# Four moves in a hand-written instruction order: gated lows, weight scales, first nested pieces, value rows

## The chip, the cores and the metric

The kernel runs on one core of one Trainium2 chip. A core has five engines that work beside each other: TensorE (PE, matmuls), VectorE (DVE), ScalarE (ACT), GpSimd (POOL) and SyncE (SP, which issues the transfers here). Each takes its instructions in program order and waits by semaphores for the others. The metric is the time of one execution on the device, in microseconds (us); lower is better.

## What is computed

A token-wise gate mixes an attention with memory and a gated feed-forward network, over the same input of 2048 tokens with 576 features:

```python
x = A_x                                              # (1, 2048, 576)
g = _sigmoid((x * gate_w).sum(-1, keepdims=True))
a = _A_ref(x, A_wq, A_wk, A_wv, A_wo, A_beta)        # 32 heads of 18, 4 segments of 512
b = (_gelu(x @ w_gate) * (x @ w_up)) @ w_down        # 576 -> 4608 -> 576
return g * a + (1 - g) * b

# inside _A_ref, per segment s, with phi(t) = t + 1 for t > 0, exp(t) otherwise:
p = softmax(qs @ ks.T * scale + mask)                # 512 x 512 per head
o = gh * ((phi(qs) @ M) / (phi(qs) @ z + 1e-6)) + (1 - gh) * (p @ vs)   # gh = sigmoid(beta), per head
M = M + phi(ks).T @ vs
z = z + phi(ks).sum(over tokens)
```

All inputs are float32. The kernel keeps each float32 operand as a pair of float16, a high and a low half, and multiplies high by high, high by low and low by high.

## The kernel before

The order of the instructions on PE, DVE, ACT and POOL is the order in which the kernel writes them; no scheduler moves anything. So a line of code that stands later is issued later on its engine, and everything behind it on that engine waits with it.

The kernel has three parts. First come the **projections**: for each of four chunks of 512 tokens (`s` 0 to 3), nine products for queries and keys (`project(s, j)`, 14 matmuls each, `chain_w`) and the rows of the values (`vrows`, evicted by `put_rows`). In chunk 0 the weights' pairs are made beside them: `make_qk` and `make_v` scale a weight, take its high half on ACT and its low half on DVE (L115) or on POOL (L606). What `put_columns` and `put_rows` leave in the list `later` is issued by `finish_later`.

Then come 72 **steps** (`step(v)`), four to a block (`fb` the block, `i4` the step in it). A step computes half of the gate and up products of one slice of 128 hidden features for 1024 tokens, by a product scheme with seven instead of eight products (names such as A11, S1, S4, written by `product` and `rest` into the accumulator banks V, X and Y); in half of them one of the products is itself split the same way (`nest`, pieces 0 to 3, and `nest_last`). Between the products stand, for one head and one half of the tokens, the scores (`scores`, L1158, evicted by `put`, which adds the mask and takes the maximum, L1161), the powers (`powers`: ACT takes the exponential and a high half `ph`, POOL a low half `pb`, L1179, and SP issues two transposing transfers into `pt`, L1182), the values (`values`, L1196, which reads `pt`) and `normalize`; and the down products of the block before (`down`, one chain of six matmuls at L1243 into a bank, evicted by DVE at L1251). A step's eight chains are `early` 0 to 4 and `late` 0 to 2. Blocks after the first take 75.6 us each, from about 262 us on. A **tail** with the output projection ends the kernel.

Four places concern the change:

- `hidden_pair` turns a gated product (`gl` or `hold`) into a pair `hh`: ACT takes the high half (L1273), POOL the low half (L1281). In a block's fourth step the low halves are only put on a list and are issued by `hidden_lows`, which stands behind `powers`. The tile `hold` is written again by the copy at L1381, after piece 0 of the nest.
- `scales(fb + 1)` sums the squares of the next block's weights over partitions by a matmul with ones (`sums`, L94) into a bank, and DVE makes powers of two of them (L265 to L272); `scales_out` goes on with six small operations on POOL (L278 to L286). The banks called `dn` are two, and taken in turn by the scores, the down chains and `sums`.
- In step 3 (the last of the first block) the four pieces of the next block's first nest stand in one step.
- In chunk 0, `make_v(2)` and `make_v(3)` go by POOL, and the three small operations on `gh` (L958 to L960) stand on DVE in the third projection.

Of the kernel before, what the change touches and what calls it, by code (L numbers as in the profile page):

```python
# [13 lines left out]
OP = mybir.AluOpType  # L14
# [4 lines left out]
P = 128  # L19
# [24 lines left out]
def kernel(ctx: ExitStack, tc: tile.TileContext, xs, wqk, wv, wo, wgu, wd, beta, out):  # L44
# [76 lines left out]
    def outscale(c, i):  # L121
        o = slice(i, i + 1)
        pool.tensor_scalar(al[:, c, o], wis[:, i if i < 2 else 4 :][:, :1], xis[:, c : c + 1], None, OP.mult)
        if i != 1:
            pool.tensor_scalar(nal[:, c, i // 2 : i // 2 + 1], al[:, c, o], -1.0, None, OP.mult)
        if i == 0:
            pool.tensor_scalar(esc[:, 0, c : c + 1], al[:, c, o], al[:, c, o], SCALE * 2.0**28, OP.mult, OP.mult)
            pool.tensor_scalar(esc[:, 1, c : c + 1], esc[:, 0, c : c + 1], -1.0, None, OP.mult)
        if i == 1:
            pool.tensor_scalar(gha[:, c], gh[:, 1], al[:, c, o], 2.0**14, OP.mult, OP.mult)  # L130

    x_raw = {}
    x16 = {}
# [266 lines left out]

    def chain_w(o, w, x, between=None):

        todo = [(k, a, 4 * b + k) for k in range(4) for a, b in ((0, 0), (0, 1), (1, 0))] + [(4, a, 8) for a in (0, 1)]
        if between:
            todo.sort(key=lambda t: (t[0] == 4, t[2] >= 4, t[1]))
        for n, (k, a, i) in enumerate(todo):
            if between and n == 8:
                between()
            pe.matmul(o, w(k, a), x[:, i], start=n == 0, stop=n == 13)  # L409

# [141 lines left out]
    with tc.tile_pool(name="prj", bufs=2, side="right", reuse_waits="tile") as pp:  # L552
# [45 lines left out]
        def make_v(k):  # L598
            t = W[9 + k] = pa.tile([P, 2, D + 2], F16, name="wv", bufs=5)
            r, sc = raw_v[:, k], wsc[:, 1:2]  # L600
            if k not in (2, 3):
                pair_of(t, r, sc)
                return
            act.activation(r, r, AF.Copy, scale=sc)
            act.activation(t[:, 0], r, AF.Copy)
            pool.tensor_tensor(t[:, 1], r, t[:, 0], OP.subtract)  # L606
# [12 lines left out]

        def project(s, j, between=None):  # L620
            w = W[j]
            i = j % 4
            if s == 0:
                i = (1, 1, 3, 4, 4, 1, 0, 3, 1)[j]
            pr = bank("dn", 2) if s and j == 0 or i == 4 else bank("G") if i == 0 else bank("U") if i == 3 else bank("st", 2)
            chain_w(pr, lambda k, a: w[:, a, k * P : (k + 1) * P], x16[s], between)
            return s, j, pr

        def put_columns(s, j, pr):
# [163 lines left out]
        with tc.manual_schedule(engines=ORDERED):  # L793
# [128 lines left out]
            def beside_products(s, j):  # L922
# [4 lines left out]
                if s == 0:  # L927
                    if j == 0:
                        put_rows(0, 0, 0, va[0], usc, 1.0)
                        make_qk(3, pair_high)  # L930
                        finish_later()
                        make_qk(3, pair_low)
                        fold_squares(0, 0)
                    if j == 1:
                        scale_sum(0, wst[:, 10:19], va[3][:, 420:])
                        turns.update(of=3, n=4)
                        dve.tensor_scalar(unq, wis[:, 4:5], 2.0**-14, wsc[:, 0:1], OP.mult, OP.mult)
                        outscale(0, 0)
                        outscale(0, 2)
                        fold_squares(0, 1)  # L940
                        make_qk(4)
                        put_rows(0, 1, 0, va[1], usc, 1.0)
                        finish_later()
                    if j == 4:
                        make_qk(7, pair_high)
                        finish_later()
                        make_qk(7, pair_low)
                    elif 2 <= j < 6:
                        make_qk(j + 3)
                    if j == 2:  # L950
                        for q in (2, 3):
                            put_rows(0, q, 0, va[q], usc, 1.0)
                        for q in FIRST:
                            put_rows(0, q, 1, vb[q], usc, 1.0)
                        finish_later()
                        x_raw.pop(0)
                    if j == 2:
                        dve.tensor_scalar(gh[:, 1], gh[:, 1], 1.0, None, OP.add)  # L958
                        dve.reciprocal(gh[:, 0], gh[:, 1])
                        dve.tensor_scalar(gh[:, 1], gh[:, 0], -1.0, 1.0, OP.mult, OP.add)  # L960
                    if j == 4:
                        outscale(0, 1)
                    if 1 <= j < 5:
                        make_v(j - 1)
                    if j == 4:
                        make_v(4)
                if s < 3:
# [46 lines left out]
            for s in range(4):  # L1014
# [26 lines left out]
                for j in range(9):  # L1041
                    if j == 1 and s:
                        make_gate(s)
                    if s and j == 0:
                        memory_scale(p)
                    pr = project(s, j, None if s or j else lambda: first_words(vb, 1, 4, FIRST))
                    if s and j == 0:
# [16 lines left out]
                    beside_products(s, j)  # L1064
                    finish_later()
                    if (s, j) == (1, 3):
                        make_gate(0)
                    if s == 0 and j >= 6:
                        q = j - 5
                        pv = vrows(0, q, 1)  # L1070
                        put_rows(0, q, 1, *pv)
                    if s == 3 and j == 6:
# [19 lines left out]
    with tc.tile_pool(name="keep", bufs=2, side="right", reuse_waits="tile") as kp, ExitStack() as tail:  # L1092
# [174 lines left out]

        lows = []

        def hidden_pair(f, c, t, wait=False):  # L1270
            slot = hh_slot[f, c] = hh_free.pop(0)
            hh = hp[f, c] = hh_tile(slot)
            act.activation(hh[:, 0], t, AF.Copy)  # L1273
            lows.append((hh, t))
            if not wait:
                hidden_lows()

        def hidden_lows():
            while lows:
                hh, t = lows.pop(0)  # L1280
                pool.tensor_tensor(hh[:, 1], t, hh[:, 0], OP.subtract)  # L1281

# [22 lines left out]
        def weights_nest(fb, i4, at):  # L1305
# [12 lines left out]
            if i4 == 2 and at == 2:  # L1318
                for i in (2,) if fb else (2, 3):
                    nest_pairs(fb + 1, i, "hl")  # L1320
            if i4 == 3 and at == 0:
                hidden_lows()
                if fb:
                    nest_pairs(fb + 1, 3, "hl")

# [76 lines left out]

        def end_pair(wait=False):

            for i, g in enumerate(ends):
                if len(g) < 5:
                    hidden(*g)
                if i == 0:
                    for qi in (1, 0):
                        if puts:  # L1410
                            puts[max(puts)](qi)
            for f, c, o, g, *_ in ends:
                hidden_pair(f, c, g, wait)
            ends.clear()

        def step(v):
# [13 lines left out]
            x1, x2_, t = x16[c], x16[e], xt[p]  # L1430
            end_pair(i4 == 3 and fb > 0)
            if v == 3:
# [9 lines left out]
            elif i4 < 2:  # L1442
                if on(k - 2):
                    values(2 * k - 3)
                V, g1 = nested.pop((fb, p)), gl_tile()
            else:
                V, g1 = bank("V"), holds[p]
                product(V, f, A22, x2_, 0, 4, True)
            X, Y = bank("G"), bank("U")
            product(X, f, A11, x1, 0, 4, True)  # L1450
            if fb and i4 < 2:
                nest_last(fb, V, p)
# [12 lines left out]
            if v == 1:  # L1465
                scale_result()
            one = 2 if fb and i4 < 2 else 1
            some(fb - 1, early[:one])
            put(2 * k - 1, 2)
# [50 lines left out]
            rest(X, f, U4, x1, (0,) if fb else (0, 1))  # L1520
            if v == 3:
                nest(at, 0)
            some(fb - 1, early[2:3])
            if fb and i4 == 1:
                scales(fb + 1)
                scales_out(fb + 1)
            product(Y, f, S1, t, 0, 2)
            rest(Y, f, G4, x2_, (0,) if fb else (0, 1))
            if v == 3:
                nest(at, 1)  # L1530
            if fb:
# [10 lines left out]
            some(fb - 1, early[3:])  # L1542
            put(2 * k, 3)
            if on(k - 2) and not on(k):
                normalize(k - 2)
            if not fb:
                hidden(f, c, X, g0)
                hidden_pair(f, c, g0, v == 2)
                if v < 3:
# [7 lines left out]
            if v == 3:  # L1557
                nest(at, 2)
            rest(Y, f, UG, x2_, (0,) if fb else (0, 1))
# [22 lines left out]
            if on(k):  # L1582
                puts[2 * k + 1] = scores(2 * k + 1)
            nest(at, 3)
            ends.append((f, e, Y, g1))
            if v == 3:
                nest_pairs_x(1, 1)
            weights_nest(fb, i4, 2)
            if v == 2:
                hidden_lows()  # L1590
            load_head(k + 2)
# [262 lines left out]
```

## Time and profile before

| | |
|---|---|
| three runs | 1621.01, 1622.6, 1622.64 us (median 1622.6) |
| the profiled execution | 1622.98 us, of which the span of the profile is 1621.3 us |
| granted TensorE clock, mean | 0.996 |
| busy: PE, DVE, ACT, POOL | 1564.1, 1275.8, 1211.2, 1124.0 us |
| transfers | 209.97 MB, 130 GB/s on the mean |

Times in the rows of a profile are microseconds from the start of the span. A row of the timeline gives the start, the length, the engine, the line of the kernel, the operation, the tile written and the tiles read, and in brackets how long the engine had waited and what released it; "x2" stands for two instructions of the same kind behind each other. A row of the waits gives the engine and its line, what it waited for, the sum, how often, and the longest.

### The profile page before, as it was taken

How to read it: one execution, taken by the hardware profiler on the slowest of the kernel's cores; microseconds unless marked ns; L12 is line 12 of the kernel's file. 1: busy time of each engine (PE TensorE's matmuls, PEld its weight loads, DVE VectorE, ACT ScalarE, POOL GpSimd, SP SyncE). 2: the span in 40 equal slices, each digit the busy share in tenths (PEclk: the TensorE clock that was granted, in tenths of full speed). 3: DMA queues.
4: the chain of work that ended last, by engine and by line, in shares of the span. 5: the costliest groups of instructions: out<-in, count | busy, mean ns of one | idle time of the engine just before them, and what ended most of it. 6: DMA issues, size and time to landing. Idle time of an engine off the chain costs nothing.

```text
span 1621.3 us, 33956 instructions
## 1 busy us (share of the span) xinstructions
PE 1564.1 (96%) x12220; PEld 957.2 (59%) x12220; DVE 1275.8 (79%) x3254; ACT 1211.2 (75%) x2059; POOL 1124.0 (69%) x1220
## 2 busy tenths in 40 slices
PE   9999999999999999999999999999999999999999
PEld 5665655555555555556555555556555556556577
DVE  6778976878878787878787878778787878787665
ACT  7567544888888887888788888887888878787421
POOL 5245555867776867686776777776868676776597
PEclk9999999999999999999999999999999999999999
DMA  6633331576867687776667677777687777764546
GB/s 222 209 129 130 123 115 55 116 131 120 145 116 148 128 123 136 121 129 130 126 119 128 121 144 121 139 121 151 119 139 130 133 127 134 121 120 95 111 85 172
DMA packets 472833, 209.97 MB, mean 130 GB/s; under 512 B 427688, under 2 KB 437416, under 8 KB 472152
## 3 DMA queue, kind: packets, MB, share of 16 engines
q1 hardware_dynamic: 472664, 207.80, 64.3%
q8 instruction: 96, 1.57, 0.4%
q14 instruction: 73, 0.60, 0.1%
HBM read 91.87 MB, written 27.26 MB: 73 GB/s over the span
## 4 chain that ended last, share of the span: by engine, by line
PE 71%; DVE 9%; POOL 8%; ACT 5%; issue 3%; DMA 3%; SPq 0%; DVEq 0%; POOLq 0%; ACTq 0%
PE dn L1243 19%; PE U L529 12%; PE G L529 8%; PE V L529 5%; PE V L1365 4%; PE pv L1196 4%; POOL pb L1179 3%; PE st L409 2%; PE dn L416 2%; DVE pb L270 1%; PE U L1289 1%; PE G L1294 1%; PE G L409 1%; PE U L409 1%; ACT ph L1178 1%
## 5 line engine op out<-in xcount | busy, mean ns | idle before, releaser
L1179 POOL TENSOR_TENSOR pb<-pb,ph 128x896 f16<-128x896 f32 (+1 forms) x256 | 368.7, 1440 | 311.7 <-ACT ph L1178 301.7
L529 PEld LDWEIGHTS <-pairg 128*128 128x128 f16 x2592 | 248.3, 98 | 260.2 <-issue 14.0
L1243 PE MATMUL dn<-paird,hhr 128*128 128x288 f16 x2124 | 327.9, 288 | 4.7 <-DVE mx L1161 4.1
L1177 ACT ACTIVATE pb<-pb,mb,esc 128x512 f32<-128x512 f32 (+3 forms) x512 | 304.9, 642 | 5.3
L1251 DVE SCALAR_TENSOR_TENSOR acc<-dn,ev,acc 128x288 f32<-128x288 f32 x534 | 263.7, 513 | 39.1 <-PE dn L1243 33.1
L1243 PEld LDWEIGHTS <-hhr 128*128 128x128 f16 x2160 | 208.3, 98 | 90.3 <-issue 19.6
L529 PE MATMUL U<-xt,pairg 128*128 128x512 f16 x864 | 209.8, 379 | 1.3 <-DVE gl L1501 1.3
L529 PE MATMUL G<-x,pairg 128*128 128x512 f16 x864 | 209.9, 379 | 0.8 <-DVE gl L1266 0.6
L1243 PE MATMUL dn<-paird,hhd 128*128 128x288 f16 x1272 | 206.3, 288 | 1.9 <-DVE mx L1161 1.9
L1178 ACT ACTIVATE ph<-pb 128x896 f16<-128x896 f32 (+1 forms) x256 | 188.5, 736 | 8.1
L342 POOL TENSOR_TENSOR pairg<-raw,pairg 128x384 f16<-128x384 f32 (+2 forms) x144 | 157.6, 1115 | 14.1 <-ACT pairg L338 14.1
L1161 DVE CUSTOM_DVE_ANT_0 pb<-st,mask 128x512 f32<-128x512 f32 (+1 forms) x256 | 157.0, 613 | 1.1 <-DMA pt<-pb 1.1
L1243 PEld LDWEIGHTS <-hhd 128*128 128x128 f16 x1296 | 125.4, 98 | 52.1 <-issue 8.5
L1365 PE MATMUL V<-xt,nest 128*128 128x256 f16 x714 | 107.1, 275 | 38.0 <-DVE hold L1381 37.7
L1172 ACT ACTIVATE mb<-mx,esc 128x4 f32<-128x4 f32 x128 | 37.1, 289 | 115.6 <-DVE mx L1161 115.6
L1161 DVE CUSTOM_DVE_ANT_0 pb<-dn,mask 128x256 f32<-128x256 f32 (+1 forms) x192 | 66.9, 373 | 67.1 <-PE dn L1158 65.1
L1365 PEld LDWEIGHTS <-nest 128*128 128x128 f16 x714 | 65.0, 98 | 73.1 <-issue 50.2
L529 PE MATMUL U<-x,pairg 128*128 128x512 f16 x432 | 105.0, 379 | 1.6 <-DVE gl L1536 1.6
L529 PE MATMUL V<-x,pairg 128*128 128x512 f16 x426 | 103.9, 380 | 0.0
L1284 ACT ACTIVATE gl<-gl,sc 128x512 f32<-128x512 f32 x110 | 75.8, 715 | 31.2 <-DVE gl L1536 19.4
L1281 POOL TENSOR_TENSOR hhr<-gl,hhr 128x512 f16<-128x512 f32 x67 | 78.4, 1180 | 14.6 <-ACT hhr L1273 14.6
L1196 PEld LDWEIGHTS <-pt 128*128 128x128 f16 x2560 | 84.2, 96 | 6.5 <-DMA pt<-pb 0.5
(364 smaller groups left out, 3142.2 us busy)
## 6 DMA issues: line engine op xcount, KB each, us to landing
raw<-in_wgu_dram SPq DMA_DIRECT2D x36, 640.0 KB
rawd<-in_wd_dram SPq DMA_DIRECT2D x36, 288.0 KB
qt<-qk SPq DMA_DIRECT2D x132, 72.0 KB
kt<-qk SPq DMA_DIRECT2D x132, 72.0 KB
qk<-stage SPq DMA_DIRECT2D x36, 256.0 KB
qt<-qk SPq DMA_DIRECT2D x132, 36.0 KB
kt<-qk SPq DMA_DIRECT2D x132, 36.0 KB
vp<-vstage SPq DMA_DIRECT2D x16, 296.0 KB
```

What stands on the lines that cost most here:

```text
L342: pool.tensor_tensor(spot(f, *p, 1), raw_g[f][:, p[0] : p[1]], spot(f, *p, 0), OP.subtract)
L529: pe.matmul(o, w[:, i, (a + k) * P : (a + k + 1) * P], x[:, b + k], start=start and k == 0 and i == 0 and b == h, stop=k == 1 and i == 1, ...
L1161: dve.tensor_tensor_reduce(scored(a, qi), out[qi], mask[:, L - (qi + 1) * P :], 1.0, -3e38, OP.add, OP.max, mx[a][:, qi : qi + 1])
L1177: act.activation(r, r, AF.Exp, bias=b[:, qi : qi + 1], scale=esc[:, 0, c : c + 1])
L1178: act.activation(h[:, cols], p, AF.Copy)
L1179: pool.tensor_tensor(low[:, cols], p, h[:, cols], OP.subtract)
L1196: pe.matmul(ov, pr[:, 10 * i + COL[qi] // P + kb], v[:, 4 * e + kb, c0 : c0 + VC], start=kb == 0 and i == 0, stop=kb == qi and i == 1)
L1243: pe.matmul(o[:, :NH], hh[:, a, q * P : (q + 1) * P], w[:, b, n * NH : (n + 1) * NH], start=i == 0, stop=i == 5)
L1251: dve.scalar_tensor_tensor(av, o[:, :NH], ev, av, OP.mult, OP.add)
L1281: pool.tensor_tensor(hh[:, 1], t, hh[:, 0], OP.subtract)
L1284: act.activation(t, o, AF.Gelu_apprx_tanh, scale=scl[f // 2][0][:, 2 + c : 3 + c])
L1365: pe.matmul(o, w[:, (7 * c + i) * P : (7 * c + i + 1) * P], x[d], start=start and n == 0, stop=n == 2, skip_group_check=True)
```

## The change

The gated lows are issued by `hidden_pair` itself, so in a block's fourth step they stand ahead of the powers' lows. `scales` and `scales_out` of a block's second step go behind the scores' evictions and two more down chains, right ahead of product S4. In step 3, piece 0 of the nest goes behind product S1 and piece 1 behind S4, and pieces 2 and 3 go into step 4, among the down chains. In chunk 0, the first four matmuls of the second projection are issued inside the first (`part`, `begun`; the order of the first eight matmuls changes with it), the second halves of the values' rows come one projection later, `make_v` is spread over five projections with only k = 3 and 4 on POOL, and the `gh` operations move to chunk 1. No matmul is added or removed.

The diff, cut to these parts:

```diff
@@ -398,15 +401,15 @@
-    def chain_w(o, w, x, between=None):
+    def chain_w(o, w, x, between=None, part=slice(0, 14)):
         todo = [(k, a, 4 * b + k) for k in range(4) for a, b in ((0, 0), (0, 1), (1, 0))] + [(4, a, 8) for a in (0, 1)]
-        if between:
-            todo.sort(key=lambda t: (t[0] == 4, t[2] >= 4, t[1]))
-        for n, (k, a, i) in enumerate(todo):
+        if between or part != slice(0, 14):
+            todo.sort(key=lambda t: (t[0] == 4, t[2] >= 4, t[1], -(t[2] // 6) if 4 <= t[2] < 8 else 0))
+        for n, (k, a, i) in list(enumerate(todo))[part]:
             if between and n == 8:
                 between()
-            pe.matmul(o, w(k, a), x[:, i], start=n == 0, stop=n == 13)
+            pe.matmul(o, w(k, a), x[:, i], start=n == 0, stop=n == 13, skip_group_check=True)
@@ -598,7 +601,7 @@
             r, sc = raw_v[:, k], wsc[:, 1:2]
-            if k not in (2, 3):
+            if k < 3:
                 pair_of(t, r, sc)
@@ -617,14 +620,25 @@
-        def project(s, j, between=None):
+        begun = {}
+
+        def project(s, j, between=None, part=slice(0, 14)):
             w = W[j]
                 i = (1, 1, 3, 4, 4, 1, 0, 3, 1)[j]
-            pr = bank("dn", 2) if s and j == 0 or i == 4 else bank("G") if i == 0 else bank("U") if i == 3 else bank("st", 2)
-            chain_w(pr, lambda k, a: w[:, a, k * P : (k + 1) * P], x16[s], between)
+            if (s, j) in begun:
+                pr, part = begun.pop((s, j)), slice(4, 14)
+            else:
+                pr = bank("dn", 2) if s and j == 0 or i == 4 else bank("G") if i == 0 else bank("U") if i == 3 else bank("st", 2)
+            chain_w(pr, lambda k, a: w[:, a, k * P : (k + 1) * P], x16[s], between, part)
+            if part == slice(0, 4):
+                begun[s, j] = pr
             return s, j, pr
+
+        def between_first():
+            first_words(vb, 1, 4, FIRST)
+            project(0, 1, None, slice(0, 4))
@@ -941,11 +955,7 @@
                         finish_later()
-                    if j == 4:
-                        make_qk(7, pair_high)
-                        finish_later()
-                        make_qk(7, pair_low)
-                    elif 2 <= j < 6:
+                    if 2 <= j < 6:
                         make_qk(j + 3)
@@ -954,16 +964,10 @@
                         x_raw.pop(0)
-                    if j == 2:
-                        dve.tensor_scalar(gh[:, 1], gh[:, 1], 1.0, None, OP.add)
-                        dve.reciprocal(gh[:, 0], gh[:, 1])
-                        dve.tensor_scalar(gh[:, 1], gh[:, 0], -1.0, 1.0, OP.mult, OP.add)
                     if j == 4:
                         outscale(0, 1)
-                    if 1 <= j < 5:
+                    if 1 <= j < 6:
                         make_v(j - 1)
-                    if j == 4:
-                        make_v(4)
                 if s < 3:
@@ -1041,9 +1045,18 @@
                         make_gate(s)
+                    if j == 1 and s == 1:
+                        dve.tensor_scalar(gh[:, 1], gh[:, 1], 1.0, None, OP.add)
+                        dve.reciprocal(gh[:, 0], gh[:, 1])
+                        dve.tensor_scalar(gh[:, 1], gh[:, 0], -1.0, 1.0, OP.mult, OP.add)
+                        gate_scale(0)
+                        gate_scale(1)
                     if s and j == 0:
                         memory_scale(p)
-                    pr = project(s, j, None if s or j else lambda: first_words(vb, 1, 4, FIRST))
+                    pr = project(s, j, None if s or j else between_first)
+                    if s == 0 and j > 6:
+                        put_rows(0, j - 6, 1, *vrows(0, j - 6, 1))
+                        later.pop()()
                     if s and j == 0:
@@ -1062,13 +1075,13 @@
                     beside_products(s, j)
-                    finish_later()
+                    if (s, j) != (0, 8):
+                        finish_later()
                     if (s, j) == (1, 3):
                         make_gate(0)
-                    if s == 0 and j >= 6:
-                        q = j - 5
-                        pv = vrows(0, q, 1)
-                        put_rows(0, q, 1, *pv)
+                    if s == 0 and j == 8:
+                        put_rows(0, 3, 1, *vrows(0, 3, 1))
+                        later.insert(0, later.pop())
                     if s == 3 and j == 6:
@@ -1265,20 +1278,11 @@
-        lows = []
-
-        def hidden_pair(f, c, t, wait=False):
+        def hidden_pair(f, c, t):
             slot = hh_slot[f, c] = hh_free.pop(0)
             act.activation(hh[:, 0], t, AF.Copy)
-            lows.append((hh, t))
-            if not wait:
-                hidden_lows()
-
-        def hidden_lows():
-            while lows:
-                hh, t = lows.pop(0)
-                pool.tensor_tensor(hh[:, 1], t, hh[:, 0], OP.subtract)
+            pool.tensor_tensor(hh[:, 1], t, hh[:, 0], OP.subtract)
@@ -1318,10 +1322,8 @@
                     nest_pairs(fb + 1, i, "hl")
-            if i4 == 3 and at == 0:
-                hidden_lows()
-                if fb:
-                    nest_pairs(fb + 1, 3, "hl")
+            if i4 == 3 and at == 0 and fb:
+                nest_pairs(fb + 1, 3, "hl")
@@ -1442,13 +1444,21 @@
                     values(2 * k - 3)
-                V, g1 = nested.pop((fb, p)), gl_tile()
+                V, g1 = nested[fb, p], gl_tile()
             else:
             product(X, f, A11, x1, 0, 4, True)
-            if fb and i4 < 2:
+            one = (2 if fb and i4 < 2 else 1) + (v == 4)
+            if v == 4:
+                dve.tensor_copy(Y, X)
+                for i in (2, 3):
+                    nest((1, 0), i)
+                    some(0, early[i - 2 : i - 1])
+                nest_last(fb, V, p)
+                dve.tensor_copy(g1, V)
+            elif fb and i4 < 2:
                 nest_last(fb, V, p)
@@ -1464,8 +1474,7 @@
                 scale_result()
-            one = 2 if fb and i4 < 2 else 1
-            some(fb - 1, early[:one])
+            some(fb - 1, early[2 * (v == 4) : one])
             put(2 * k - 1, 2)
@@ -1518,16 +1527,11 @@
             rest(X, f, U4, x1, (0,) if fb else (0, 1))
-            if v == 3:
-                nest(at, 0)
-            some(fb - 1, early[2:3])
-            if fb and i4 == 1:
-                scales(fb + 1)
-                scales_out(fb + 1)
+            some(fb - 1, early[max(one, 2):3])
             product(Y, f, S1, t, 0, 2)
             if v == 3:
-                nest(at, 1)
+                nest(at, 0)
             if fb:
@@ -1541,11 +1545,14 @@
             put(2 * k, 3)
+            if fb and i4 == 1:
+                scales(fb + 1)
+                scales_out(fb + 1)
             if on(k - 2) and not on(k):
                 hidden(f, c, X, g0)
-                hidden_pair(f, c, g0, v == 2)
+                hidden_pair(f, c, g0)
                 if v < 3:
@@ -1555,7 +1562,7 @@
             if v == 3:
-                nest(at, 2)
+                nest(at, 1)
             rest(Y, f, UG, x2_, (0,) if fb else (0, 1))
@@ -1581,13 +1588,12 @@
                 puts[2 * k + 1] = scores(2 * k + 1)
-            nest(at, 3)
+            if v != 3:
+                nest(at, 3)
             ends.append((f, e, Y, g1))
             weights_nest(fb, i4, 2)
-            if v == 2:
-                hidden_lows()
             load_head(k + 2)
                 load_v((k + 2) // 4)
```

On POOL, in the fourth step of a block, `pb` are the powers' lows, `hhr` and `nest` the gated lows and the nested weights. Before:

```order
L1179 TENSOR_TENSOR pb_4798<-pb_4799,ph 128x384
L377 TENSOR_TENSOR nest<-nest 128x256
L1179 TENSOR_TENSOR pb_4912<-pb_4912,ph 128x896
L1179 TENSOR_TENSOR pb_4912<-pb_4913,ph 128x384
L1281 TENSOR_TENSOR hhr_4940<-gl,hhr_4940 128x512
L1281 TENSOR_TENSOR hhr_4942<-hold_3983,hhr_4942 128x512
L377 TENSOR_TENSOR nest<-raw,nest 128x256
L342 TENSOR_TENSOR pairg<-raw,pairg 128x384
```

and after:

```order
L1192 TENSOR_TENSOR pb_4798<-pb_4799,ph 128x384
L380 TENSOR_TENSOR nest<-nest 128x256
L1285 TENSOR_TENSOR hhr_4940<-gl,hhr_4940 128x512
L1285 TENSOR_TENSOR hhr_4943<-hold_3983,hhr_4943 128x512
L1192 TENSOR_TENSOR pb_4912<-pb_4912,ph 128x896
L1192 TENSOR_TENSOR pb_4912<-pb_4913,ph 128x384
L380 TENSOR_TENSOR nest<-raw,nest 128x256
L345 TENSOR_TENSOR pairg<-raw,pairg 128x384
```

The two `hhr` rows went ahead of the two rows that read `ph`.

On PE, in the second step of a block, the rows around `sums` (`stat` is its operand). Before:

```order
L1243 LDWEIGHTS hhd_3818
L1243 MATMUL dn<-paird,hhd_3818 128x288
L1243 LDWEIGHTS hhd_3818
L1243 MATMUL dn<-paird,hhd_3818 128x288
L94 MATMUL dn<-stat_89,ones 128x10
L529 LDWEIGHTS pairg
L529 MATMUL U<-xt_2333,pairg 128x512
L529 LDWEIGHTS pairg
```

and after:

```order
L1256 LDWEIGHTS hhd_3819
L1256 MATMUL dn<-paird,hhd_3819 128x288
L1256 LDWEIGHTS hhd_3819
L1256 MATMUL dn<-paird,hhd_3819 128x288
L94 MATMUL dn<-stat_89,ones 128x10
L532 LDWEIGHTS pairg
L532 MATMUL U<-x_1750,pairg 128x512
L532 LDWEIGHTS pairg
```

`sums` went from the product that reads `xt` (S1) to the one that reads `x` (S4). The chain ahead of it is now the second of two behind the scores.

On DVE, in the same step, `mx` is the maximum of the scores, `acc` a down chain's eviction, and `z`, `v`, and `pb` without a number the scales' chain. Before:

```order
L1251 SCALAR_TENSOR_TENSOR acc<-dn,ev,acc 128x288
L265 TENSOR_REDUCE z<-dn 128x2
L266 TENSOR_SCALAR z<-x_78,z 128x4
L269 TENSOR_SCALAR v<-z 128x2
L270 TENSOR_SCALAR pb<-z 128x4
L271 TENSOR_SCALAR v<-v 128x2
L272 TENSOR_SCALAR pb<-pb 128x4
L1161 ISA pb_9030,mx<-dn,mask 128x256
L1161 ISA mx 128x1
L1536 TENSOR_TENSOR gl<-U,gl 128x512
```

and after:

```order
L1174 ISA mx 128x1
L1264 SCALAR_TENSOR_TENSOR acc<-dn,ev,acc 128x288 x2
L1174 ISA pb_9009,mx<-st,mask 128x512
L1174 ISA mx 128x1
L268 TENSOR_REDUCE z<-dn 128x2
L269 TENSOR_SCALAR z<-x_78,z 128x4
L272 TENSOR_SCALAR v<-z 128x2
L273 TENSOR_SCALAR pb<-z 128x4
L274 TENSOR_SCALAR v<-v 128x2
L275 TENSOR_SCALAR pb<-pb 128x4
L1264 SCALAR_TENSOR_TENSOR acc<-dn,ev,acc 128x288
L1174 ISA pb_9009,mx<-st,mask 128x384
```

The scales' chain went from ahead of the scores' first eviction to between the evictions of the two wide ones, `st`.

More of the change, by code (lines that the diff above doesn't have):

```diff
@@ L128, in outscale, with gate_scale @@
             pool.tensor_scalar(esc[:, 1, c : c + 1], esc[:, 0, c : c + 1], -1.0, None, OP.mult)
-        if i == 1:
-            pool.tensor_scalar(gha[:, c], gh[:, 1], al[:, c, o], 2.0**14, OP.mult, OP.mult)
+        if i == 1 and c > 1:
+            gate_scale(c)
+    def gate_scale(c):
+        pool.tensor_scalar(gha[:, c], gh[:, 1], al[:, c, 1:2], 2.0**14, OP.mult, OP.mult)
     x_raw = {}
@@ L1401, in end_first, with end_pair @@
             ends[0] = ends[0] + (True,)
-        def end_pair(wait=False):
+        def end_pair():
             for i, g in enumerate(ends):
@@ L1412, in end_pair @@
             for f, c, o, g, *_ in ends:
-                hidden_pair(f, c, g, wait)
+                hidden_pair(f, c, g)
             ends.clear()
@@ L1430, in step @@
             x1, x2_, t = x16[c], x16[e], xt[p]
-            end_pair(i4 == 3 and fb > 0)
+            end_pair()
             if v == 3:
```

## The prediction

> **What bounds the kernel now.** I read the profile's page first, then the list of waits, then the timeline around the longest one.
>
> ```profile
> PE 1564.1 (96%) x12220; PEld 957.2 (59%) x12220; DVE 1275.8 (79%) x3254; ACT 1211.2 (75%) x2059; POOL 1124.0 (69%) x1220
> ```
>
> TensorE (PE) is busy for 1564.1 of 1621.3 us, and the change adds and removes no matmul, so it can move only the time in which PE stands still or runs slowly. The list of waits says where PE stands still (us in total, times, longest):
>
> ```profile
> PE V L1365 <- DVE hold L1381: 37.7, 16, 2.5
> PE dn L1243 <- DVE mx L1161: 5.9, 16, 1.0
> PE U L529 <- DVE gl L1536: 1.6, 1, 1.6
> PE U L529 <- DVE gl L1501: 1.3, 1, 1.3
> PE G L409 <- DVE wp L115: 1.2, 1, 1.2
> PE dn L416 <- ACT stage L634: 1.2, 1, 1.2
> DVE hold L1381 <- POOL hhd L1281: 31.3, 11, 3.0
> DVE hold L1381 <- POOL hhr L1281: 15.0, 5, 3.0
> ```
>
> The first row is two thirds of all that can be won: in 16 blocks PE waits for the copy of `hold`, and the last two rows say that this copy waits in the same 16 for POOL's low half of `hold`. This is one of the sixteen, in the fourth step of a block (start, length; what an engine waited for is in brackets):
>
> ```profile
> 703.41 0.61 ACT L1273 ACTIVATE hhd<-hold 128x512 f16<-128x512 f32 x1
> 705.69 0.95 ACT L1178 ACTIVATE ph<-pb 128x896 f16<-128x896 f32 x1
> ...
> 704.16 0.67 POOL L377 TENSOR_TENSOR nest<-nest 128x256 f16<-128x256 f32 x1
> 706.72 2.88 POOL L1179 TENSOR_TENSOR pb<-pb,ph 128x896 f16<-128x896 f32 x2 [1.89 <-ACT ph L1178]
> 709.56 1.15 POOL L1281 TENSOR_TENSOR hhd<-gl,hhd 128x512 f16<-128x512 f32 x1
> 710.67 1.15 POOL L1281 TENSOR_TENSOR hhd<-hold,hhd 128x512 f16<-128x512 f32 x1
> ...
> 711.86 0.42 DVE L1381 COPY hold<-V 128x256 f32<-128x256 f32 x1 [3.00 <-POOL hhd L1281]
> ...
> 709.35 0.53 PE L1243 MATMUL dn<-paird,hhr 128*128 128x288 f16 x3
> 712.34 0.49 PE L1365 MATMUL V<-xt,nest 128*128 128x256 f16 x3 [2.45 <-DVE hold L1381]
> 716.32 0.66 PE L1196 MATMUL pv<-vt,pt 128*128 128x37 f16 x20
> ...
> 710.11 2.94 SPq L1182 DMA_TRANSPOSE pt<-pb  x1
> ```
>
> POOL idles for 1.89 us before the powers' lows (L1179), although both gated high halves were there when ACT ended at 703.41 + 0.61 = 704.02. The gated lows then stand behind 2.88 us of powers' lows.
>
> **The change, part by part. The gated lows sooner.** They go ahead of the powers' lows. They can run from 704.83 (end of L377), and 2.3 us of work ends at about 707.1, while DVE is free for the copy from 711.86 - 3.00 = 708.86 and PE is at the down chains until 709.88. So the sixteen waits go: **-37.7**. The bill goes to the powers' lows, which start at 707.1 instead of 706.72: 0.4 later, and so does the transposing transfer that SP issues behind them.
>
> These waits have a second cost. Four of them are followed by a stretch in which PE runs at half clock (columns: window, length, busy time of each engine, PEclk, DMA share, GB/s):
>
> ```profile
> core 0: us, PE busy (x) PEld busy (x) DVE busy (x) ACT busy (x) POOL busy (x), PEclk, DMA share, GB/s
> 635.35:638.76 3.41, 3.41 (x23) 2.27 (x22) 1.97 (x7) 2.65 (x5) 3.41 (x4) 0.50 0.60 127
> 1321.43:1324.84 3.41, 3.41 (x34) 2.29 (x31) 1.50 (x4) 3.30 (x5) 3.41 (x3) 0.50 0.59 144
> ...
> 635.16 0.65 PE L1365 MATMUL V<-xt,nest 128*128 128x256 f16 x3 [2.45 <-DVE hold L1381]
> 1320.38 0.49 PE L1365 MATMUL V<-xt,nest 128*128 128x256 f16 x3 [2.47 <-DVE hold L1381]
> ```
>
> These rows are the first and the last of the four. Each slow stretch begins 0.2 to 1.1 us after such a wait ends, and none stands elsewhere; the shorter waits (1.6 us and less) are followed by none. Four stretches of 3.41 us at half speed cost 4 x 1.7 = 6.8 us, and they go with the waits: **-6.8**. The Trainium skill ("TensorE: Matmul & The Clock Gate", section "HAM oscillation — how this bites in real kernels") has the rule "no PE-idle gaps >~3.4µs". By that rule a 2.45 us wait would not lower the clock, the slow stretches would have another cause, and the sum would be 6.8 higher. Here the row differs from the rule, and I go by the row.
>
> **The scales later.** Today the matmul `sums` (L94) stands before the scores in the second step, and its DVE chain delays the scores' eviction:
>
> ```profile
> 672.19 0.90 PE L1243 MATMUL dn<-paird,hhr 128*128 128x288 f16 x6 [0.29 <-DVE mx L1161]
> ...
> 669.68 2.90 POOL L1179 TENSOR_TENSOR pb<-pb,ph 128x896 f16<-128x896 f32 x2 [0.22 <-ACT ph L1178]
> 669.79 1.80 DVE L270 TENSOR_SCALAR pb<-z 128x4 int32<-128x4 int32 x1
> 671.71 0.42 DVE L1161 CUSTOM_DVE_ANT_0 pb<-dn,mask 128x256 f32<-128x256 f32 x1
> ...
> 651.61 1.65 PE L1243 MATMUL dn<-paird,hhr 128*128 128x288 f16 x12
> 653.09 1.46 PE L529 MATMUL U<-x,pairg 128*128 128x512 f16 x6
> ...
> 653.58 0.94 DVE L1251 SCALAR_TENSOR_TENSOR acc<-dn,ev,acc 128x288 f32<-128x288 f32 x2
> ...
> 674.53 0.23 POOL L278 TENSOR_SCALAR sc<-v 128x2 f32<-128x2 f32 x1
> 675.37 0.52 DVE L1251 SCALAR_TENSOR_TENSOR acc<-dn,ev,acc 128x288 f32<-128x288 f32 x1 [0.37 <-PE dn L1243]
> 676.39 0.30 ACT L1172 ACTIVATE mb<-mx,esc 128x4 f32<-128x4 f32 x1 [1.11 <-DVE mx L1161]
> ```
>
> That is the 5.9 us of the second row of the waits, and it goes: **-5.9**. But in its new place `sums` stands directly behind two down chains and takes the `dn` bank of the first of them, so it must wait for that chain's eviction (L1251). The rows from 651.61 to 653.58 show the same place in the first step of a block, which has no `sums`: PE is through with the two chains (12 matmuls from 651.61) at 653.09, and DVE finishes the first of its two evictions at 653.58 + 0.47 = 654.05. There PE goes on with another bank; now it would stand for 0.96 us, and 1.0 with the signal (0.06 from the end of the copy of `hold`, 712.28, to PE's 712.34). Behind `sums` on PE stands the whole product S4. Seventeen steps have it: 17 x 1.0 = **+17.0** (bounds 0, if the bank came free otherwise, and +25, if it waits for both evictions). Its DVE chain then lies beside S4, in the gap ahead of the eviction that waits for PE at 675.37. Today the chain takes 2.4 us, 1.8 of them in the one operation that starts just after POOL's L1179 and ends with its first half. In the new place POOL has nothing but the scales' own operations (674.53), which wait for this chain, so I take it at under 1 us, and hidden. If it stays slow, it passes on up to 0.9 us to the maximum that ACT waits for at 676.39, and by it to the powers' chain below.
>
> **What is late next.** PE comes 2.46 us sooner to `values` (716.32, L1196), which reads the transposed powers `pt`. The chain to `pt` (ACT, POOL, SP) does not come sooner: it runs from the maximum at 676.39 on without waiting for PE, and POOL's part is now 0.4 later. PE would be there at 713.86. The page doesn't say when `pt` lands; the rows bound it. It cannot land before its issue ends, 710.11 + 2.94 + 0.4 = 713.45, and then nobody waits. It has landed by 716.32, where PE waits in no block, which makes 716.32 + 0.4 - 713.86 = 2.86 at most. So 0 to 2.86 a block, 0 to +45.8 in all. Other issues are shorter and longer, and one landing elsewhere on the critical chain was long:
>
> ```profile
> 632.46 2.56 SPq L1182 DMA_TRANSPOSE pt<-pb  x1
> 988.09 8.35 DMA pt<-pb
> ```
>
> The first ends 0.14 us before that block's wait does, where the one at 710.11 ended 0.71 after. Taking 0.4 of the earlier end into account, the middle of the bounds (1.4) falls to 1.0: 16 x 1.0 = **+16**.
>
> **The parts that run once.** In the projections the sixth weight's low half and the values' rows make PE wait 1.2 us each; in steps 3 and 4 the nest does.
>
> ```profile
> 37.61 1.90 DVE L115 SCALAR_TENSOR_TENSOR wp<-acc,wsc,wp 128x640 f16<-128x640 f32 x1
> 253.87 0.69 DVE L1501 COPY gl<-U 128x512 f32<-128x512 f32 x1 [5.19 <-POOL hhd L1281]
> 261.89 1.28 DVE L480 SCALAR_TENSOR_TENSOR xt<-acc,xsc,xt 128x1024 f16<-128x1024 f32 x1
> ```
>
> The gate's three small operations and one weight's low half leave DVE ahead of 37.61, and the rows come a projection later, so both waits should go; with 0.2 for a later piece that waits for the eviction of the bank begun early: **-2.2** (bounds -2.4 and 0, DVE being without a break there). In steps 3 and 4 the two waits of 1.6 and 1.3 go, but the nest's first copy now stands ahead of the addition that the last product of step 3 waits for (as 1.3 long as the wait it replaces), and the xt conversion of 1.28 now stands ahead of the nest's additions in step 4 (0.8): -2.9 + 1.3 + 0.8 = **-0.8** (bounds -2.9 and +0.5).
>
> **Sum.** -37.7 - 6.8 - 5.9 + 17.0 + 16 - 2.2 - 0.8 = -20.4. The profiled execution took 1622.98 us, so 1602.6; the median of the runs is 0.4 lower, and I say 1602.
>
> **Rivals.**
> - *The transposes land in time.* Then the +16 is missing: 1586.6. For it: 20 matmuls and 2.9 us lie between today's issue end and 716.32. Against it: the issue alone ends at 713.45, 0.4 before PE arrives. If `sums` doesn't wait either (it does if the bank is taken as written), 1569.6.
> - *The half clock stays*, since the four stretches have another cause than the wait: 1609.4. Against it: all four follow the removed wait. The page's rule above gives this case.
> - *The wait is moved whole.* If `pt` lands at the upper bound in every block, PE stands 2.86 us at `values`, the low clock may follow that wait as it followed the old one, and the sum is -37.7 + 45.8 - 5.9 + 17.0 - 2.2 - 0.8 = +16.2: 1639.2, slower. It decides at a mean wait of (37.7 + 5.9 + 2.2 + 0.8 - 17.0) / 16 = 1.85 us (2.3 if the half clock goes nevertheless). For it: the landing of 8.35 us. Against it: that one includes an issue, and 716.32 shows no wait in any block.
> - *Nothing moves*, because POOL's lows still start late: 1622.
>
> **Chances.** Main 0.64; transposes in time 0.15 and neither new wait 0.04; half clock stays 0.04; moved whole 0.08; nothing 0.05. The range is 1583 to 1618: it leaves out the case without either wait, most of the moved wait and the case in which nothing moves (0.17 together); the main case alone has 1592 to 1612 (0.4 to 1.6 us at `values`). A measurement of this kernel tells 0.2% (3.2 us) from no change: faster 0.88, same 0.05, slower 0.07.
>
> **What would show it.** The row of `hold` must be gone from the waits, and the slow stretches with it. L94 must have a wait of about 1 us, 17 times, released by a down chain's eviction, and the row of mx must be gone. `values` must show 16 new waits of about 1 us, released by `pt`. I am wrong if `hold` still waits, if the 17 waits are missing, or if `values` waits for more than 1.85 us.

## The result, and the profile after

The changed kernel took 1605.27 us (median of 4 runs, 1601.08 to 1607.38) against 1622.62 us before: a ratio of 0.9892, with a 95% interval from 0.987 to 0.9914. The forecast was 1602 us in a range of 1583 to 1618. The profiled execution is the fastest of the four, 1601.08 us with a span of 1599.3, so the two profiles differ by 22 us and the medians by 17.

The page's first rows and the largest rows of the waits, in the changed kernel (lines have moved: L1367 is the former L1365, L1383 the copy of `hold`, L1264 the former L1251, L1209 the values):

```profile
PE 1561.1 (98%) x12220; PEld 955.8 (60%) x12220; DVE 1250.5 (78%) x3254; ACT 1208.3 (76%) x2059; POOL 1127.7 (71%) x1220
...
PE dn L94 <- DVE acc L1264: 13.5, 16, 0.9
PE pv L1209 <- DMA pt<-pb: 12.5, 13, 2.3
PE V L1367 <- DVE hold L1391: 1.5, 2, 1.3
PE pv L1209 <- DMA pt<-ph: 1.2, 2, 1.1
PE U L532 <- DVE gl L1540: 1.1, 1, 1.1
...
PE dn L94 <- DVE acc L1262: 0.9, 1, 0.9
PE st L412 <- DVE wp L115: 0.8, 1, 0.8
...
PE dn L1256 <- DVE mx L1174: 0.2, 1, 0.2
```

The row of 37.7 us is gone, and that of `mx` has fallen from 5.9 to 0.2. In their place stand `sums` (L94), which did not wait before and now waits 17 times, 14.4 us in all, and the values, which wait 15 times for `pt`, 13.7 us (one wait of 0.3 us before).

The fourth step of the same block as was shown of before:

```profile
697.36 1.16 POOL L1285 TENSOR_TENSOR hhd<-gl,hhd 128x512 f16<-128x512 f32 x1
698.47 1.17 POOL L1285 TENSOR_TENSOR hhd<-hold,hhd 128x512 f16<-128x512 f32 x1
699.59 2.89 POOL L1192 TENSOR_TENSOR pb<-pb,ph 128x896 f16<-128x896 f32 x2
...
701.82 0.42 DVE L1383 COPY hold<-V 128x256 f32<-128x256 f32 x1 [0.39 <-PE V L1367]
...
702.30 0.49 PE L1367 MATMUL V<-xt,nest 128*128 128x256 f16 x3
...
702.51 2.43 SPq L1195 DMA_TRANSPOSE pt<-pb  x1
...
706.28 0.18 PE L1209 MATMUL pv<-vt,pt 128*128 128x37 f16 x1
707.07 0.59 PE L1209 MATMUL pv<-vt,pt 128*128 128x37 f16 x17 [0.61 <-DMA pt<-pb]
```

The gated lows run first, the copy of `hold` waits for PE and no longer for POOL, and the nest's matmuls at 702.30 start without a wait. Then the bill: the values start at 706.28 on the high halves and stand 0.61 us for the low ones, whose issue ended at 704.94.

The second step, with `sums` in its new place:

```profile
662.75 1.65 PE L1256 MATMUL dn<-paird,hhr 128*128 128x288 f16 x12
665.27 0.36 PE L94 MATMUL dn<-stat,ones 128*128 128x10 f32 x2 [0.88 <-DVE acc L1264]
...
664.61 0.94 DVE L1264 SCALAR_TENSOR_TENSOR acc<-dn,ev,acc 128x288 f32<-128x288 f32 x2
666.53 0.17 DVE L273 TENSOR_SCALAR pb<-z 128x4 int32<-128x4 int32 x1
667.93 0.52 DVE L1264 SCALAR_TENSOR_TENSOR acc<-dn,ev,acc 128x288 f32<-128x288 f32 x1 [1.02 <-PE dn L1256]
```

The first of the two evictions ends about 665.08, and `sums` follows. The scales' chain lies in DVE's idle time, and its slow operation takes 0.17 us here instead of 1.80.

One half-clock stretch is left (columns as in the prediction). It starts 0.1 us after the longest wait of the profile, 2.34 us at the values, has ended:

```profile
556.22:559.63 3.41, 3.41 (x27) 1.65 (x27) 0.00 (x0) 2.44 (x6) 3.25 (x3) 0.50 1.53 356
...
556.11 0.75 PE L1209 MATMUL pv<-vt,pt 128*128 128x37 f16 x19 [2.34 <-DMA pt<-pb]
```

### The profile page after: what moved, and what is told of

Its sections match the earlier page's. It is cut to its first block, busy times and chain, and to the rows that moved or that the text cites. A ratio compares the mean times of both kernels' runs of the same rounds, so it can differ in the third digit from the quotient of the medians.

```text
span 1599.3 us, 33926 instructions
## 1 busy us (share of the span) xinstructions
PE 1561.1 (98%) x12220; PEld 955.8 (60%) x12220; DVE 1250.5 (78%) x3254; ACT 1208.3 (76%) x2059; POOL 1127.7 (71%) x1220
## 4 chain that ended last, share of the span: by engine, by line
PE 71%; POOL 12%; DMA 6%; DVE 5%; ACT 3%; issue 2%; SPq 0%; DVEq 0%; POOLq 0%; ACTq 0%
PE dn L1256 17%; PE U L532 13%; PE G L532 9%; POOL pb L1192 5%; DMA pt<-pb 5%; PE V L532 4%; PE pv L1209 3%; PE V L1367 3%; PE st L412 3%; PE dn L419 2%; PE U L1293 2%; ACT pb L1190 2%; PE U L412 2%; PE G L412 1%; POOL hhr L1285 1%
## 5 line engine op out<-in xcount | busy, mean ns | idle before, releaser
L1256 PE MATMUL dn<-paird,hhr 128*128 128x288 f16 x2124 | 324.2, 286 | 0.4 <-DVE acc L1264 0.4
L1264 DVE SCALAR_TENSOR_TENSOR acc<-dn,ev,acc 128x288 f32<-128x288 f32 x534 | 263.3, 513 | 48.5 <-PE dn L1256 42.6
L1367 PE MATMUL V<-xt,nest 128*128 128x256 f16 x714 | 106.1, 273 | 1.5 <-DVE hold L1391 1.5
L1209 PE MATMUL pv<-vt,pt 128*128 128x37 f16 x2560 | 87.3, 179 | 13.9 <-DMA pt<-pb 12.5
L1209 PEld LDWEIGHTS <-pt 128*128 128x128 f16 x2560 | 83.4, 96 | 22.5 <-DMA pt<-pb 15.0
```

Source lines behind the costliest of these rows:

```text
L1209: pe.matmul(ov, pr[:, 10 * i + COL[qi] // P + kb], v[:, 4 * e + kb, c0 : c0 + VC], start=kb == 0 and i == 0, stop=kb == qi and i == 1)
L1256: pe.matmul(o[:, :NH], hh[:, a, q * P : (q + 1) * P], w[:, b, n * NH : (n + 1) * NH], start=i == 0, stop=i == 5)
L1264: dve.scalar_tensor_tensor(av, o[:, :NH], ev, av, OP.mult, OP.add)
L1367: pe.matmul(o, w[:, (7 * c + i) * P : (7 * c + i + 1) * P], x[d], start=start and n == 0, stop=n == 2, skip_group_check=True)
```

## The experiments

The first three runs take parts of the change back. With the kernel before and the changed one they make the four corners of lows (a) and scales (b); the parts that run once stay in all three.

**Lows put back.** In `hidden_pair` the low half goes back on the list, and `hidden_lows` stands again behind `powers` (main lines):

```diff
-            pool.tensor_tensor(hh[:, 1], t, hh[:, 0], OP.subtract)
+            lows.append((hh, t))
+            if not wait:
+                hidden_lows()
...
-            if i4 == 3 and at == 0 and fb:
-                nest_pairs(fb + 1, 3, "hl")
+            if i4 == 3 and at == 0:
+                hidden_lows()
+                if fb:
+                    nest_pairs(fb + 1, 3, "hl")
...
-            end_pair()
+            end_pair(i4 == 3 and fb > 0)
```

> The changed kernel with the gated lows put back behind the powers' lows in a block's fourth step. My theory: the 16 waits of 2.46 us at the copy of hold come back (+39), the waits at values and most of the waits for pt go (-14), and some half-clock stretches come back (+2 to +9): 1605 + 28 to 34, so about 1636 us, with the row of sums (14 us) unchanged. Rival: the lows are not what the time came from, and the time stays within 8 us of 1605.

Measured: 1638.67 us (1635.38 to 1639.94), ratio to before 1.0103 (1.0084 to 1.0122). The waits of PE and the mean clock:

```profile
PE V L1378 <- DVE hold L1394: 37.4, 16, 2.5
PE dn L94 <- DVE acc L1264: 13.5, 16, 0.9
...
core 0: 1633.7 us, clock 0.993
```

The 16 waits are back, no row of `pt` is left among the waits, and the time is 33.4 us above that of the changed kernel: the first theory, and a kernel slower than before, since the scales' cost stands without the lows' gain. The clock of 0.993 is seven half-clock stretches of 3.41 us where the kernel before had four (0.996); the other three runs have clocks of 0.990 and 0.991.

**Scales put back.**

```diff
             some(fb - 1, early[max(one, 2):3])
+            if fb and i4 == 1:
+                scales(fb + 1)
+                scales_out(fb + 1)
             product(Y, f, S1, t, 0, 2)
...
             put(2 * k, 3)
-            if fb and i4 == 1:
-                scales(fb + 1)
-                scales_out(fb + 1)
```

> The changed kernel with the scales put back ahead of product S1 in a block's second step. My theory: 17 waits of 0.88 us at sums go (-15), and 16 waits of 0.3 to 0.4 us at the scores' eviction come back (+6): about 1596 us. Rival: the wait at sums only takes time that PE would wait later anyway (at values, for pt), so that the time stays at 1605 and the row of pt grows by some 9 us.

Measured: 1593.2 us (1591.07 to 1595.92), ratio 0.9821 (0.9803 to 0.9839).

```profile
PE pv L1209 <- DMA pt<-pb: 14.1, 15, 2.4
PE dn L1256 <- DVE mx L1174: 5.3, 16, 0.9
...
PE pv L1209 <- DMA pt<-ph: 0.9, 1, 0.9
```

The row of `sums` is gone, that of `mx` is back, and those of `pt` make 15.0 us instead of 13.7. So the wait at `sums` did not shield the values: moving the scales cost 12.1 us between the medians (9.4 between the two profiled executions, which have one half-clock stretch each), and part (b) of the change is a loss by itself.

**Both put back.** Both edits above together, which leaves the parts that run once.

> The changed kernel with the lows and the scales both put back, so that only the parts that run once are left (projections, first nest). My theory: 2 to 3 us below the kernel before, about 1620 us. Rival: the parts that run once bring nothing or cost something, 1622 to 1625 us; or they carry much of the gain, below 1616 us.

Measured: 1620.77 us (1616.89 to 1623.89, 12 runs), ratio 0.9988 (0.9978 to 0.9998). That is 1.9 us less than before, with an interval from 0.3 to 3.6. These parts bring something, and little.

**The scales behind S4.** The same three lines, moved from ahead of product S4 to behind it:

```diff
             put(2 * k, 3)
-            if fb and i4 == 1:
-                scales(fb + 1)
-                scales_out(fb + 1)
...
             product(Y, f, S4, x2_, 2, 6)
             if v == 3:
                 nest(at, 1)
             rest(Y, f, UG, x2_, (0,) if fb else (0, 1))
+            if fb and i4 == 1:
+                scales(fb + 1)
+                scales_out(fb + 1)
```

> The changed kernel with the scales behind product S4 instead of ahead of it. My theory: PE gets the bank without waiting, since the eviction ends during S4, and all 17 waits go: about 1590 us. Rival: the scales' chain on DVE now delays the maximum that the powers wait for, pt lands later and the row of pt grows by 8 us or more: 1598 us or above.

Measured: 1587.26 us (1582.97 to 1589.47), ratio 0.978 (0.9761 to 0.9799). The waits, and the place in the second step:

```profile
PE pv L1209 <- DMA pt<-pb: 13.3, 15, 2.4
PE V L1367 <- DVE hold L1391: 1.4, 2, 1.3
...
657.69 1.46 PE L532 MATMUL U<-x,pairg 128*128 128x512 f16 x6
659.20 0.29 PE L94 MATMUL dn<-stat,ones 128*128 128x10 f32 x2
```

S4 covers the eviction, `sums` starts without a wait, and the waits for `pt` stay (13.9 us with those for its high halves, against 13.7). Of `sums` no row is left, and of `mx` 0.2 us: 18.0 us below the changed kernel. Of the 18.0 us between the profiled spans, 14.4 are waits, and PE's busy time is 4.1 shorter, 1.7 of that for the half-clock stretch, which this execution lacks; the other 2.4 no row shown here explains.

**The values later.** In a block's first step `values(2k-3)` goes behind two down chains:

```diff
             elif i4 < 2:
-                if on(k - 2):
+                if on(k - 2) and i4 == 1:
                     values(2 * k - 3)
...
-            if on(k - 2) and not (fb and i4 < 2):
+            if on(k - 2) and not (fb and i4 == 1):
                 values(2 * k - 3)
```

> The changed kernel with the values of a block's first step moved behind the first two down chains of that step (as they stand in its third and fourth step), so that pt has some 4 us more to land. My theory: the 13.7 us of waits for pt at values go, and the half clock that may follow the longest of them: 1605 - 13.7 = about 1591 us, with the row of sums unchanged. Rival: the wait moves on to what follows values (the normalizing on DVE, the accumulator pv, the next scores) and the time stays above 1600 us.

Measured: 1590.46 us (1589.54 to 1591.35), ratio 0.9803 (0.9789 to 0.9816).

```profile
PE dn L94 <- DVE acc L1264: 12.6, 15, 0.9
PE G L532 <- DVE gl L1279: 3.8, 18, 0.4
PE pv L1209 <- DMA pt<-pb: 2.2, 3, 1.0
...
core 0: 1589.6 us, clock 1.000
```

The waits for `pt` fall from 13.7 to 2.2 us. A new small row appears (3.8 us at the copy of a gated product), and the time falls by 14.8 us. The five runs lie within 1.8 us, those of the changed kernel within 6.3, and the granted clock is 1.000 in all five, against 0.996 to 0.999.

**Both mends together.**

> The changed kernel with the scales behind product S4 and with the values of a block's first step behind two down chains. My theory: the two gains add, since they lie at different places of a block and both are PE's own waits: 1587.3 - 13.3 = about 1574 us, with all waits of PE together under 10 us. Rival: with PE 29 us sooner another engine or transfer ends last (ACT's powers, POOL's lows, the loads) and shows as a new row of over 5 us: 1579 us or above.

Measured: 1572.67 us (1571.43 to 1574.77), ratio 0.9696 (0.9683 to 0.9709), the fastest version here.

```profile
PE 1556.1 (99%) x12220; PEld 955.9 (61%) x12220; DVE 1247.0 (79%) x3254; ACT 1208.5 (77%) x2059; POOL 1129.0 (72%) x1220
...
PE G L532 <- DVE gl L1279: 4.0, 19, 0.4
PE pv L1209 <- DMA pt<-pb: 3.0, 3, 1.5
PE V L1367 <- DVE hold L1391: 1.5, 2, 1.3
...
core 0: 1572.0 us, clock 1.000
```

The two gains add (18.0 + 14.8 = 32.8; measured 32.6). PE is at work for 1556.1 of 1572.0 us at full clock, and no row of the waits is above 4 us. The expectation that all waits together stay under 10 us was missed by a little: the rows of the list make about 12.

**A shorter wait at `hold`.** Only the low half of `hold` goes behind the powers' lows again; that of `gl` stays ahead. The list is as in the first experiment, and the condition holds for the second tile alone:

```diff
-            for f, c, o, g, *_ in ends:
-                hidden_pair(f, c, g)
+            for n, (f, c, o, g, *_) in enumerate(ends):
+                hidden_pair(f, c, g, wait and n == 1)
```

> The changed kernel with only the low half of gl ahead of the powers' lows and that of hold still behind them, which makes the wait at hold shorter and not nothing: POOL's low of hold then ends one 1.15 us operation earlier than in the kernel before, so 16 waits of about 1.3 us (21 us). My theory: the half clock needs a wait of about 2.3 us or more, so that no half-clock stretch follows these; waits for pt fall to under 3 us; time about 1605 + 21 - 12 = 1614 us. Rival: any regular wait can bring the half clock, and four to seven stretches of 3.4 us (7 to 12 us of time) stand behind the sixteen as before: 1621 us or above.

Measured: 1608.38 us (1607.57 to 1610.12), ratio 0.9916 (0.9903 to 0.993).

```profile
PE V L1378 <- DVE hold L1394: 20.2, 16, 1.4
PE dn L94 <- DVE acc L1264: 13.5, 16, 0.9
PE pv L1209 <- DMA pt<-pb: 2.6, 6, 1.3
...
core 0: 1606.3 us, clock 1.000
```

Sixteen waits stand at the same place, thirteen of 1.34 to 1.37 us and three shorter (in the kernel before 13 of them were 2.4 to 2.5 us long), and not one half-clock stretch follows. The waits for `pt` fall as expected, because PE comes later. The time is 6 us below what I expected, because I started from the changed kernel's median, in which the half clock has a part that is absent here; from its profiled execution the rows add up: 1601.1 + 20.2 - (13.7 - 2.6) - 1.7 for the half clock = 1608.5.

## Why the prediction was right

**The lows (-37.7, then +16).** Both halves held. The wait at `hold` vanished entirely (37.7 to nothing), and the wait at the values came, 13.7 us in 15 waits (13 blocks) against the forecast's 16 us in 16. The bounds, 0 to 2.86 us a block, hold every one: the longest is 2.34. That the mean of 0.9 us lies near the forecast's 1.0, the middle of bounds read from one block, is in part luck: three waits, of 1.84, 2.30 and 2.34 us, make nearly half of the sum, and three blocks have none. The way from 37.7 to a net of about 24 is therefore shown, by the lows put back (37.4 us at `hold` and none for `pt`) and by the values moved: when PE has other work there, the waits fall to 2.2 us. The rival "transposes land in time" fell on the 15 waits for `pt`; "the wait is moved whole" fell on their mean of 0.9 us.

**The half clock (-6.8).** This is the term that was most off. The sum took four stretches away; the profile after has one, so 5.1 us in that execution. But it is the fastest of the four, with a clock of 0.999; the others have 0.996, 0.996 and 0.998. A stretch of 3.41 us at 0.50 lowers a run's mean clock by 0.001 and costs 1.7 us, so a run's span times (1 - clock) is an estimate of what it lost (to about 0.8 us a run, as the clock is given to 0.001):

| kernel (runs) | mean span | lost at half clock | rest |
|---|---|---|---|
| before (17, beside the first experiments) | 1621.1 | 7.7 | 1613.4 |
| both put back (12) | 1619.2 | 8.1 | 1611.1 |
| scales put back (4) | 1591.6 | 2.8 | 1588.8 |
| lows put back (4) | 1636.5 | 14.7 | 1621.7 |
| changed (4) | 1603.0 | 4.4 | 1598.6 |

So only about 3.3 of the 6.8 us came, by four runs of the changed kernel. The step that was too simple was to count the removed waits only: the new waits at the values reach 2.3 us, and one of these is followed by a stretch in the profile too. That these are the place is shown by the runs that shorten them: with the values moved, with both mends, and with only the low of `hold` behind, PE has no wait above 1.5 us in the profile, and all 13 runs have a clock of 1.000. The rule from the Trainium skill, by which the stretches had another cause and would stay, is refuted by the two ends: with the long waits back, they come back (seven; five with both edits put back, clock 0.994), with waits of up to 1.4 us at the same place there is none.

**The scales (+17.0 - 5.9).** The wait at `sums` is where it was put, 17 times, sixteen of them of 0.88 us instead of 1.0: 14.4. The row of `mx` fell by 5.7. The net of +8.7 by the rows is 12.1 us between the medians (1605.27 against 1593.2). Of the difference of 3.4, about 1.6 is the half clock (4.4 against 2.8 in the table); the rest is not shown. That the scales' chain would be short and hidden held too: 0.17 us for the operation that took 1.80, and the chain ends at 666.91, ahead of the eviction at 667.93.

**The parts that run once (-3.0).** Measured by the run with both edits put back: -1.9 (0.3 to 3.6 of gain). In the projections the two waits of 1.2 us went, and one of 0.8 came (L412); in steps 3 and 4, 1.6 and 1.3 became 1.1 and 1.3. Which of them brings what is below what these runs can tell.

**The sum.** Between the two profiled spans (22.0 us apart), all waits of PE added over the whole lists fall from 52.8 to 34.1 us, which is 18.7, and PE's busy time falls by 3.0. Three stretches fewer make 5.1 of busy time, so PE's other work rose by about 2.1, which no row explains. The medians differ by 17.35 and the mean spans in the table by 18.1. Part by part, with the half clock taken out as in the table, the lows bring 22.3 us with the scales at their old place and 23.1 at the new one (forecast 37.7 - 16 = 21.7), the scales cost 9.8 and 10.6 (17.0 - 5.9 = 11.1), and the parts that run once bring 2.3 (3.0). So the mechanism held for all of them, and the sizes within 1.5 us; the forecast came out 3 us low, about as much as the half clock fell short. It also makes the spread: without it the spans of the changed kernel's four runs lie between 1597.7 and 1599.3 us, with it between 1599.3 and 1605.7.

## What to carry to other kernels

A wait that is taken away on the busiest engine is worth its length less what the next consumer then waits for: look for what that engine reads next and which chain makes it, and bound the new wait by the rows of issue and arrival. Before an instruction is put behind others, ask whose buffer it takes: here a matmul of 0.3 us took the bank of a chain just ended, and one product further on the same instruction cost nothing. When several edits go together, measure them apart: one of these was a loss of 12 us inside a gain of 17. And read the granted clock of every run, not only of the profiled one: here it told what the runs without a trace had spent.

## What the runs showed of the hardware

The half clock depends on how long PE stands. The traces of the kernel before, of the lows put back and of both put back have 48 waits at `hold`. Of these, 38 are 2.4 to 2.5 us long, and 16 of them (4, 7 and 5) were followed by a stretch of 3.41 us at 0.50; the other ten, of 1.7 to 2.2 us, were followed by none. Of the waits for `pt` in the changed kernel, with the scales put back and with the scales behind S4, six are 2.30 to 2.36 us long, and two of these were followed. In no trace did a stretch follow a wait of 2.20 us or less, the sixteen of up to 1.4 us among them. So a wait well under 3.4 us can cost 1.7 us more than itself, here from about 2.3 us on. The chance differs from kernel to kernel: by the table above the lows put back lose 14.7 us and both put back 8.1 with waits of the same length, and why is not shown.

The Trainium skill ("TensorE: Matmul & The Clock Gate", section "What's actually happening") says that the clock is decided over a free-running window of 3413 ns. The length of the stretches agrees with that. An estimate by which a stretch comes whenever the whole wait lies inside one window would give (3.41 - 2.46) / 3.41 = 0.28 for the long waits and 0.60 for those of 1.35 us; the runs show 16 of 38 and none of 13, so the chance is counted here and not explained.

A DVE operation of 128x4 integers took 1805 ns in the middle of its 19 times before, 170 in all 19 after it was moved, and 1805 again when it was put back (minimum, median and maximum in ns; three rows, in this order):

```profile
L270 DVE TENSOR_SCALAR pb<-z x19: 156/1805/1809, 163.7 to 1505.7; 128x4 int32<-128x4 int32 x19
...
L273 DVE TENSOR_SCALAR pb<-z x19: 170/170/172, 161.2 to 1487.1; 128x4 int32<-128x4 int32 x19
...
L273 DVE TENSOR_SCALAR pb<-z x19: 170/1805/1811, 161.0 to 1474.5; 128x4 int32<-128x4 int32 x19
```

In the slow place it starts 0.1 us after POOL's L1179 and ends with that operation's first 1.89 us; in the quick place POOL waits. The Trainium skill ("Trainium Architecture — The Big Picture", section "What this means for kernel authors") says that the ports which these two engines share are held by one of them at a time. These rows agree with it, and give its price here: 1.6 us for an operation of 0.17. In two blocks of the kernel before, POOL's operation starts earlier in the chain, and another DVE operation takes the long time: L266 with 1.60 us at 591.95, L269 with 1.87 at 1430.38. Not every DVE operation beside POOL is slowed: L272, of the same 128x4 form, takes 0.17 us at 671.63, during POOL's second L1179.
